# Output weights of the second MLP kept as even columns, then odd ones, with their block sums in freed weight slots on GpSimd's DMA queue

## The chip, the cores and the metric

One Trainium2 chip, one of its cores. The metric is the device time of one execution in microseconds (us); less is better. Engines: PE multiplies matrices (PEld is its weight load, which runs beside the multiplication), DVE, ACT and POOL (GpSimd) compute elementwise, SP only starts transfers. ACT and POOL can start transfers too, each in a queue of its own. Every engine runs its instructions in the order in which they are written.

## The reference, cut to what matters

```python
x = attention(q, k, v, mem_k, mem_v)          # 3072 tokens x 512
x = (sigmoid(x @ w_gate) * (x @ w_val)) @ w_out   # first MLP, 512 -> 1536 -> 512
h = x @ w_in                                  # second MLP, 512 -> 2048
g = h * sigmoid(1.702 * h)
out = g @ w2_out                              # 2048 -> 512, float32
```

All is float32. The kernel multiplies in a shorter format: each operand is cut into a high part (a rounded copy) and a low part (what the copy lost), and a product is three matmuls, high by high, high by low, low by high.

## The kernel before, in words

The tokens are six blocks of 512. Attention and the first MLP fill the first 600 us or so; the second MLP then goes over three pairs of blocks (`sb` 0, 1, 2). Its hidden layer is made for a pair at a time by a seven-product scheme (Strassen's kind): `part_product` (L1366) multiplies weight combinations from a ring (`sb_r`, fetched from `wc_dram` by SP, L1274) with token combinations `sb_x`; ACT copies a bank away (`snap`, L1378, into `sb_s`), DVE adds another bank to the copy (`plus`, L1382), and ACT applies the gate (L1825).

The output product differs by pair:

- For `sb` 0 it is plain. `gemm4` (L790) multiplies with the 16 row blocks f of `w2_out`, once for the first 512 tokens and once for the next, the gated values cut into `gh`, `gl` (`halves`, L1393 on ACT, L1397 on DVE; two buffers of each). Each block lies in a slot of two halves, high and low. The slots of f = 3 to 10 are the two tiles `wq0`, `wq1`, four slots each. A block of the result is copied from its bank into one of two buffers `f2` (L1116, L1118) and stored by SP.
- For `sb` 1 and 2 it is the seven-product scheme again (`b_phase`, from four block pairs j at a time): `b_product` (L1712) takes as its stationary operand 128 of 256 columns of a weight combination. Half s_ = 0 takes the even columns, s_ = 1 the odd ones, so that a later transpose can write the result rows whole:

```python
lhs = w[:, wl * H2 : (wl + 1) * H2].rearrange("p (c z) -> p c z", z=2)[:, :, s_]
```

The weight combinations come from DRAM (`wo_dram`, L1668). `out2` prepares them while the hidden layer of `sb` 0 runs: it converts row block f from float64 (`convert`), keeps the float32 values in `wp_dram` (L1563), and stores three of the seven combinations, which are plain quarters. The other four (m3, m5, m6, m7) are made by `sums2(j)` for the block pairs j = 0 to 7, from the second plain pass on: two loads from `wp_dram` (L1585) into buffers of gated values that are already used up, four sums on DVE (L1594) in the one buffer `sb_t`, two cuts into high (ACT, L1608) and low (DVE, L1611), each of two combinations, and four stores (L1618). All loads and stores are on SP's queue. The first cut's buffer is the half `xl1_g[2:4]`, the second's is `f2`, for every j.

The order on each engine is set by a planner (`Schedule.run`): each step has a cost, keys it reads and writes, and a due time that follows from the products behind it; the planner plays the steps through and writes them down in the order in which it would start them. A waiting step holds everything behind it on its engine.

Of the kernel before, what the change touches and what calls it, by code (L numbers as in the profile page):

```python
# [8 lines left out]
F32 = mybir.dt.float32  # L9
# [6 lines left out]
ALU = mybir.AluOpType  # L16
# [128 lines left out]
def kernel(  # L145
# [112 lines left out]

    sraw = []

    def convert(slot, src, gate=None, put=None, only=None):
# [48 lines left out]

        def join():
            nc.vector.scalar_tensor_tensor(
                out=fi, in0=fi, scalar=3, in1=words()[:, :, 0], op0=ALU.logical_shift_left, op1=ALU.bitwise_or
            )

        def high():
            nc.scalar.activation(slots[slot][:, 0, :], ft, AF.Copy)  # L317

        def low():
            w = slots[slot]  # L320
            eng = nc.vector if low_dve else nc.gpsimd
            eng.tensor_tensor(out=w[:, 1, :], in0=ft, in1=w[:, 0, :].bitcast(F32), op=ALU.subtract)  # L322
# [766 lines left out]
    def gemm4(f, i, banks, row, end=False, tts=range(TT)):  # L1089
# [18 lines left out]
        for tt in tts:  # L1108
# [3 lines left out]
            for c in range(0, 512, h):  # L1112

                def ev(on_dve, c=slice(c, c + h), st=st, bk=bk):
                    if on_dve:
                        nc.vector.tensor_copy(st[:, c], bank[bk][:, c])  # L1116
                    else:
                        nc.scalar.activation(st[:, c], bank[bk][:, c], AF.Copy)  # L1118

                own = c > 0  # L1120

# [434 lines left out]
    def out2(a, b):  # L1556
        for f in range(a, b):
            g = nconv[0] % NF
            sl = slot_out2[f]
            convert(sl, rows(w2_out, f))  # L1560

            def park2(f=f, g=g):
                nc.sync.dma_start(out=wp_dram[f], in_=fts[g])  # L1563
# [12 lines left out]
                add("sp", 0.45, put_, r=r, w=[("wod", unit(j, m), j % 2)], nbytes=P * 512 * 4)  # L1576

    def sums2(j):
        q = 2 if j % 2 == 0 else 6
        wa, wb = (lambda: gbs[q]), (lambda: gbs[q + 1])  # L1580
        ka, kb = ("gB", q), ("gB", q + 1)
        for x in range(2):

            def load(x=x):
                nc.sync.dma_start(out=gbs[q + x], in_=wp_dram[2 * j + x])  # L1585

            add("sp", 0.45, load, r=[("wp", 2 * j + x)], w=[("gB", q + x)], nbytes=P * 512 * 4)
        lo_, hi_ = slice(0, H2), slice(H2, 2 * H2)
        t = lambda: work["t"]
        k0, k1 = ("t", 0), ("t", 1)  # L1590

        def sub(o, x, y, r, op=ALU.subtract):
            def fn():
# [4 lines left out]
        def cut(ms, b_):
            keys = [("gB", 10), ("gB", 11)] if b_ else [("f", NF), ("f", NF + 1)]
            buf = (lambda: twin["l1"][:, 2:4]) if b_ else (lambda: twin["f"])  # L1600

            def part(i, dtype):
                return buf().bitcast(dtype)[:, :, i * H2 : (i + 1) * H2]

            src = lambda: t().rearrange("p (m c) -> p m c", c=H2)
# [24 lines left out]
    GT = ("h0", "l0", "l1", "g3")  # L1630
# [273 lines left out]
```

## Time and profile before

| | us |
|---|---|
| median of three runs | 1159.66 (1158.67 to 1160.36) |
| the profiled execution | 1161.62 |
| its span, first to last instruction | 1159.8 |
| PE busy in the span | 1135.8 |
| DVE, ACT, POOL busy | 811.0, 563.7, 138.8 |

The profile times one execution. What lies outside the span is start and end of the program. Busy time is summed over instructions that overlap only in part, so a busy PE can still be a slow one; the granted clock in a stretch says at which of its two levels (1.2 and 2.4 GHz) it ran there.

### The profile page before, as it was taken

To read this page: it belongs to the slowest core of one execution; us is meant where nothing else is said; L and a number is where in the kernel's file an instruction comes from. 1 tells how busy PE (TensorE), PEld (TensorE's weight loads), DVE (VectorE), ACT (ScalarE), POOL (GpSimd) and SP (SyncE) were. 2 spreads that over 40 slices of the span, in tenths; PEclk is the share of its full clock that TensorE was granted. 3 is DMA by queue.
4 is the path that set the end of the run, shared out by engine and by line. 5 is a ranking of instruction groups with operands and counts; after the bars stand their busy time and mean duration, and the time that the engine had idled before them with its cause. 6 is when DMAs were issued, how large, how long until landed. Compare 5 with 4: busy or idle time off the path is not lost.

```text
span 1159.8 us, 19578 instructions
## 1 busy us (share of the span) xinstructions
PE 1135.8 (98%) x7230; PEld 948.5 (82%) x7230; DVE 811.0 (70%) x1405; ACT 563.7 (49%) x954; POOL 138.8 (12%) x174
## 2 busy tenths in 40 slices
PE   8999999999999999999999999999988999999997
PEld 7888899987888888888888888888866888888886
DVE  7998757776776777878866857648575469675375
ACT  6887622222222323665546677755454365354442
POOL 5322343123233111000000100000000000000000
PEclk9999999999999999999999999999998999999999
DMA  9666344335434424353337777684895576866526
GB/s 207 223 204 191 76 128 94 53 70 126 106 81 84 110 54 124 109 162 120 119 111 248 265 269 259 230 296 146 297 346 199 186 219 205 253 199 192 172 76 179
DMA packets 247791, 196.84 MB, mean 170 GB/s; under 512 B 165136, under 2 KB 191760, under 8 KB 247696
## 3 DMA queue, kind: packets, MB, share of 16 engines
q1 hardware_dynamic: 207624, 173.83, 50.2%
q10 hardware_dynamic: 38152, 15.47, 4.9%
q0 software_dynamic: 1920, 6.29, 1.4%
q8 instruction: 57, 0.93, 0.3%
q14 instruction: 38, 0.31, 0.1%
HBM read 141.00 MB, written 54.53 MB: 169 GB/s over the span
## 4 chain that ended last, share of the span: by engine, by line
PE 90%; DMA 3%; SPq 3%; DVE 1%; ACT 1%; issue 1%; ACTq 0%; DVEq 0%
PE bank L1366 29%; PE bank L1015 15%; PE bank L816 14%; PE bank L1712 14%; PE bank L790 8%; PE bank L823 7%; SPq L345 3%; PE both L699 2%; PE both L550 1%; DMA raw<-in_k_dram 1%; DMA raw<-in_moe_w_in_dram 1%; DMA raw<-in_moe_w_out_dram 0%; PE bank L699 0%; PE bank L880 0%; DMA wo_dram<-xl_g 0%
## 5 line engine op out<-in xcount | busy, mean ns | idle before, releaser
L1366 PE MATMUL bank<-sb_x,sb_r 128*128 128x512 f32 x1512 | 354.6, 393 | 10.8 <-ACT sb_s L1378 10.8
L1366 PEld LDWEIGHTS bank<-sb_x,sb_r 128*128 128x128 f32 x1512 | 286.6, 190 | 72.2 <-ACT sb_s L1378 12.3
L816 PE MATMUL bank<-xh,w 128*128 128x512 f32 (+1 forms) x464 | 159.5, 355 | 0.0
L816 PE MATMUL bank<-xl,w 128*128 128x512 f32 (+1 forms) x464 | 158.6, 353 | 0.1
L1382 DVE TENSOR_TENSOR sb_s<-bank,sb_s 128x512 f32<-128x512 f32 x108 | 74.2, 689 | 74.4 <-PE bank L1366 59.2
L1712 PE MATMUL bank<-wq,w 128*128 128x512 f32 x504 | 123.3, 394 | 0.0
L1712 PEld LDWEIGHTS bank<-wq,w 128*128 128x128 f32 x504 | 97.4, 193 | 20.3 <-ACT wq L1680 0.3
L823 PE MATMUL bank<-xh,w 128*128 128x512 f32 (+1 forms) x464 | 108.8, 356 | 0.0
L1015 PE MATMUL bank<-gh,wq 128*128 128x512 f32 (+1 forms) x448 | 98.8, 361 | 0.0
L816 PEld LDWEIGHTS bank<-xh,w 128*128 128x128 f32 x464 | 87.8, 189 | 12.7
L816 PEld LDWEIGHTS bank<-xl,w 128*128 128x128 f32 x464 | 87.8, 189 | 12.3 <-DVE xl L756 0.5
L1378 ACT ACTIVATE sb_s<-bank 128x512 f32<-128x512 f32 x108 | 64.8, 601 | 52.7 <-PE bank L1366 52.1
L823 PEld LDWEIGHTS bank<-xh,w 128*128 128x128 f32 x464 | 78.2, 189 | 12.3
L1015 PEld LDWEIGHTS bank<-gh,wq 128*128 128x128 f32 x448 | 76.4, 189 | 13.0
L665 DVE STREAM_TRANSPOSE pt<-raw 32x256 f32<-32x256 f32 x184 | 79.6, 432 | 3.7 <-POOL raw L618 1.1
L848 ACT ACTIVATE gh<-sig 128x512 fp32r<-128x512 f32 (+1 forms) x58 | 32.3, 557 | 70.1 <-DVE sig L843 61.6
L618 POOL TENSOR_TENSOR raw<-e,sm 96x448 f32<-96x448 f32 (+2 forms) x69 | 37.9, 560 | 199.3 <-DVE sm L610 163.3
L840 ACT ACTIVATE sig<-bank 128x512 f32<-128x512 f32 (+1 forms) x58 | 30.4, 524 | 61.8 <-PE bank L823 56.5
L322 POOL TENSOR_TENSOR w<-f,w 128x512 fp32r<-128x512 f32 x14 | 20.3, 1452 | 278.3 <-ACT w L317 278.1
L1015 PE MATMUL bank<-gl,wq 128*128 128x512 f32 (+1 forms) x224 | 53.4, 360 | 0.0
L843 DVE SCALAR_TENSOR_TENSOR sig<-sig,bank 128x512 f32<-128x512 f32 (+1 forms) x58 | 34.0, 587 | 26.4 <-PE bank L823 25.1
L567 DVE TENSOR_REDUCE mx<-both 96x8 f32<-96x512 f32 x32 | 21.9, 685 | 40.5 <-ACT xh L753 27.6
(221 smaller groups left out, 1817.4 us busy)
## 6 DMA issues: line engine op xcount, KB each, us to landing
sb_r<-wc_dram SPq DMA_DIRECT2D x133, 256.0 KB
w<-wo_dram SPq DMA_DIRECT2D x42, 512.0 KB
raw<-in_moe_w_out_dram SPq DMA_DIRECT2D x24, 512.0 KB
raw<-in_moe_w_in_dram SPq DMA_DIRECT2D x16, 512.0 KB
wc_dram<-sb_r SPq DMA_DIRECT2D x15, 512.0 KB
w_e<-wo_dram SPq DMA_DIRECT2D x14, 512.0 KB
wf_dram<-f POOLq DMA_DIRECT2D x24, 256.0 KB, 3.2
y_dram<-f ACTq DMA_DIRECT2D x24, 256.0 KB
```

What stands on the lines that cost most here:

```text
L345: add("pool" if pool else "act" if act else "sp", dur, lambda: q_.dma_start(out=dst(), in_=src), r=list(r), w=[key], nbytes=n)
L618: eng.tensor_tensor(out=dst, in0=e3()[r, :, c], in1=T["sm"][r].to_broadcast([n, H, keys[1] - keys[0]]), op=ALU.mult)
L665: nc.vector.transpose(T["pt"][r * CH : (r + 1) * CH, :, c * CH : (c + 1) * CH], T["pn"][c * CH : (c + 1) * CH, :, kb * CH : (kb + 1) * CH],)
L790: nc.tensor.matmul(ps_out, a, c, start=(first and i == 0 and j == 0), stop=(last and i == n - 1 and j == 2),)
L816: nc.tensor.matmul(bank[bk][:, :n], w[:, 0, ts[t]], x[xb][:, t, c0 : c0 + n], start=t == 0 and x is xhs, stop=False)
L823: nc.tensor.matmul(bank[bk][:, :n], w[:, 1, ts[t]], xhs[xb][:, t, c0 : c0 + n], start=False, stop=t == NK - 1)
L843: nc.vector.scalar_tensor_tensor(out=sig[:, :n], in0=sig[:, :n], scalar=1.0, in1=bank[src_val][:, :n], op0=ALU.add, op1=ALU.mult)
L1015: nc.tensor.matmul(bank[into[m]][:, c0 : c0 + n], w[:, wi, m * P : (m + 1) * P], g[:, :n], start=f == 0 and j == 0 and c0 == 0, stop=f == ...
L1366: nc.tensor.matmul(bank[bk], w[:, o : o + P], xt[x, k][:, xl, :], start=first and k == 0 and wl == 0 and xl == 0, stop=k == 1 and wl == 1, ...
L1378: add("act", c_act(BLK), lambda: nc.scalar.activation(work[n], bank[bk], AF.Copy), r=[("bank", bk)], w=[n])
L1382: nc.vector.tensor_tensor(out=work[n], in0=bank[bk], in1=work[n], op=ALU.add)
L1712: nc.tensor.matmul(bank[bk], lhs, quad[b_][:, x, gl_, :], start=begin, stop=last and x == js[-1] and wl == 1, skip_group_check=not first,)
```

## The change: what it does

Four edits, in one diff.

1. `convert(..., split=True)` for the blocks of `w2_out`: the high and low parts are written with the even columns of each 256 first, then the odd ones. The source is read with a step of two elements. The stationary operand of L1712 is then 128 neighbouring columns.
2. `gemm4` of `sb` 0 now yields its columns in that order, so its copies out of the banks write with a step of two elements (`apart(st)`).
3. `sums2` works in weight slots that the second plain pass has used up: j even takes the slots of f = 3 (loaded pair), 4 and 5 (cuts) with `sb_t`; j odd those of f = 6, 7 and 8 with the first gate buffer `sig` in place of `sb_t`. So there are two sets of buffers in place of one. The cuts regroup the columns, reading with a step of two.
4. The pair's two loads become one transfer of 512 KB and each cut's two stores become one of 512 KB, all on POOL's queue, with 4 us of slack in the planner's due times. That is 24 transfers for 48.

```diff
+    def apart(x):
+        return x.rearrange("p (h c s) -> p h s c", s=2, c=P)
...
         def high():
-            nc.scalar.activation(slots[slot][:, 0, :], ft, AF.Copy)
+            w, x = slots[slot][:, 0, :], ft
+            if split:
+                w, x = w.rearrange("p (h s c) -> p h s c", s=2, c=P), apart(ft)
+            nc.scalar.activation(w, x, AF.Copy)
...
+                    x = bank[bk].rearrange("p (h s c) -> p h s c", s=2, c=P)
                     if on_dve:
-                        nc.vector.tensor_copy(st[:, c], bank[bk][:, c])
+                        nc.vector.tensor_copy(apart(st), x)
...
     def sums2(j):
-        q = 2 if j % 2 == 0 else 6
-        wa, wb = (lambda: gbs[q]), (lambda: gbs[q + 1])
-        for x in range(2):
-            def load(x=x):
-                nc.sync.dma_start(out=gbs[q + x], in_=wp_dram[2 * j + x])
+        s_in, *s_out = [sl for g4 in quads4 for sl in g4][3 * (j % 2) : 3 * (j % 2) + 3]
+        def load():
+            nc.gpsimd.dma_start(out=slots[s_in].bitcast(F32), in_=wp_dram[2 * j : 2 * j + 2].rearrange("x p c -> p x c"))
+        add("pool", 1.0, load, r=[("wp", 2 * j), ("wp", 2 * j + 1)], w=wkeys(s_in), nbytes=2 * P * 512 * 4, slack=4.0)
...
-        t = lambda: work["t"]
+        t = (lambda: sigs[0]) if j % 2 else (lambda: work["t"])
...
-                def store(i=i, m=m):
-                    nc.sync.dma_start(out=wo_dram[unit(j, m)][:, j % 2, :], in_=buf()[:, i])
+            def store():
+                dst = wo_dram[u : u + d + 1 : d, :, j % 2, :].rearrange("m p c -> p m c")
+                nc.gpsimd.dma_start(out=dst, in_=slots[sl].bitcast(F32))
...
-        cut(("m5", "m6"), 1)
+        cut(("m6", "m5"), s_out[0])
...
-        cut(("m3", "m7"), 0)
+        cut(("m7", "m3"), s_out[1])
...
-                    lhs = w[:, wl * H2 : (wl + 1) * H2].rearrange("p (c z) -> p c z", z=2)[:, :, s_]
+                    lhs = w[:, wl * H2 : (wl + 1) * H2][:, s_ * P : (s_ + 1) * P]
```

Lines below L240 move down by three to eleven: L1378 becomes L1388, L1397 L1407, L1594 L1604, L1608 L1617, L1611 L1620, L1680 L1691, L1712 L1723, L1825 L1836; the loads of `sums2` are L1595 and its stores L1627. On SP, DVE and ACT nothing is in another order before the second plain pass. Three places change in what the engines wait for.

ACT, before, in the last products of `sb` 1 that come ahead of the first `b_phase` (j = 2 and 3 of the hidden layer; `sb_s` is a bank's copy, `xl_g<-sb_t` and `f<-sb_t` are cuts of `sums2`):

```order
L1825 ACTIVATE xh_g<-bank_5268 128x512
L1680 ACTIVATE wq_746<-xh_g 128x512
L1608 ACTIVATE f_83<-sb_t 128x2x256
L1608 ACTIVATE xl_g<-sb_t 128x2x256
L1825 ACTIVATE xh_g<-sb_s_5303 128x512
L1378 ACTIVATE sb_s_5303<-bank_69 128x512
L1680 ACTIVATE wq_745<-xh_g 128x512
L1825 ACTIVATE xh_g<-sb_s_5303 128x512
L1608 ACTIVATE f_83<-sb_t 128x2x256
L1680 ACTIVATE wq_745<-xh_g 128x512
L1378 ACTIVATE sb_s_5303<-bank_5268 128x512
L1608 ACTIVATE xl_g<-sb_t 128x2x256
```

ACT, in the change, around the last two cuts of `sums2` (the rows `wq_746<-sig`; `L1388` is a bank's copy, `L1836` the gate):

```order
L1388 ACTIVATE sb_s_5303<-bank_5268 128x512
L1617 ACTIVATE wq_746<-sig 128x2x256
L1836 ACTIVATE xh_g<-bank_69 128x512
L1388 ACTIVATE sb_s_5305<-bank_5269 128x512
L1617 ACTIVATE wq_746<-sig 128x2x256
L1128 ACTIVATE f_83<-bank_70 128x2x2x128
L1388 ACTIVATE sb_s_5304<-bank_5268 128x512
L1836 ACTIVATE xh_g<-sb_s_5303 128x512
L1836 ACTIVATE xl_g<-sb_s_5304 128x512
L1836 ACTIVATE xl_g<-sb_s_5305 128x512
L1388 ACTIVATE sb_s_5303<-bank_69 128x512
L1836 ACTIVATE xh_g<-bank_5268 128x512
```

Before, eight of the sixteen cuts stand behind the first `L1680` row, the cuts of the output phase; in the change all sixteen stand ahead of every `L1691` row, the last one in j = 2's products.

DVE, before, in the second plain pass, from the low part of f = 8 to that of f = 12 (`gl` is a low part; `sb_t` a sum of `sums2`):

```order
L1397 TENSOR_TENSOR gl_88<-xl_g,gh_86 128x512
L1249 TENSOR_TENSOR f_81<-sb_y_7584 128x512
L1249 TENSOR_TENSOR sb_y_7584<-sb_y_7585,sb_y_7584 128x512
L1397 TENSOR_TENSOR gl_89<-xl_g,gh_87 128x512
L1397 TENSOR_TENSOR gl_88<-xl_g,gh_86 128x512
L1397 TENSOR_TENSOR gl_89<-xl_g,gh_87 128x512
L1611 TENSOR_TENSOR xl_g<-sb_t,xl_g 128x2x256
L1594 TENSOR_TENSOR sb_t<-xh_g,sb_t 128x256
L1397 TENSOR_TENSOR gl_88<-sb_h_5436,gh_86 128x512
```

DVE, in the change, from the low part of f = 9 to that of f = 11:

```order
L1407 TENSOR_TENSOR gl_89<-xl_g,gh_87 128x512
L1259 TENSOR_TENSOR sb_y_7584<-sb_y_7585,sb_y_7584 128x512
L1604 TENSOR_TENSOR sig<-wq_745 128x256
L1407 TENSOR_TENSOR gl_88<-xl_g,gh_86 128x512
L1604 TENSOR_TENSOR sig<-sig,wq_745 128x256
L1604 TENSOR_TENSOR sb_t<-wq_745 128x256
L1604 TENSOR_TENSOR sb_t<-sb_t,wq_745 128x256
L1620 TENSOR_TENSOR wq_746<-sig,wq_746 128x2x256
L1604 TENSOR_TENSOR sig<-wq_745,sig 128x256
L1620 TENSOR_TENSOR wq_745<-sb_t,wq_745 128x2x256
L1604 TENSOR_TENSOR sig<-wq_745 128x256
L1407 TENSOR_TENSOR gl_89<-xl_g,gh_87 128x512
```

Sums of j = 1 and j = 2 now stand between the low parts that the plain pass needs, so a pair that is not loaded yet holds those up. On PE one product of `sb` 1 (`sb_x00` by `sb_r0`) moves to between f = 8 and f = 9 of the plain pass.

SP, before, near the end of the products (the fetches of `sb_r` wait for free places in the ring; stores of `sums2` between them):

```order
L1618 DMA wo_dram<-xl_g 128x512 x2
L1274 DMA sb_r_4713<-wc_dram 128x512
L1274 DMA sb_r_4464<-wc_dram 128x512
L1618 DMA wo_dram<-f_83 128x512 x2
L1274 DMA sb_r_4523<-wc_dram 128x512
L1274 DMA sb_r_4691<-wc_dram 128x512
L1618 DMA wo_dram<-xl_g 128x512 x2
```

POOL, in the change, its last rows (before, POOL ends with conversions and starts no transfer after the first MLP):

```order
L1627 DMA wo_dram<-wq_746 128x2x512
L1595 DMA wq_745<-wp_dram 128x2x512
L1627 DMA wo_dram<-wq_745 128x2x512
L1627 DMA wo_dram<-wq_746 128x2x512
L1595 DMA wq_745<-wp_dram 128x2x512
L1627 DMA wo_dram<-wq_746 128x2x512
L1627 DMA wo_dram<-wq_745 128x2x512 x2
L1627 DMA wo_dram<-wq_746 128x2x512 x2
```

The stores no longer stand behind ring fetches.

## Rows read from the trace of the kernel before

**Rows 1.** The page's head and its first part: busy us, share, instructions.
```profile
span 1159.8 us, 19578 instructions
PE 1135.8 (98%) x7230; PEld 948.5 (82%) x7230; DVE 811.0 (70%) x1405; ACT 563.7 (49%) x954; POOL 138.8 (12%) x174
```

**Rows 2.** Windows: busy us by engine, granted clock, DMA share, GB/s.
```profile
800.00:820.00 20.00, 20.00 (x90) 16.54 (x90) 12.37 (x21) 7.31 (x12) 0.00 (x0) 1.00 0.43 144
...
840.00:860.00 20.00, 20.00 (x90) 16.58 (x89) 16.07 (x24) 9.95 (x16) 0.00 (x0) 1.00 1.01 357
860.00:880.00 20.00, 9.87 (x35) 7.33 (x33) 9.86 (x18) 8.02 (x15) 0.00 (x0) 0.80 0.77 267
880.00:900.00 20.00, 19.58 (x74) 16.00 (x75) 12.67 (x14) 11.02 (x17) 0.00 (x0) 0.86 0.61 199
```

**Rows 3.** Timeline of PE: start, length, what, count, idle before and releaser.
```profile
836.30 26.00 PE L1366 MATMUL bank<-sb_x,sb_r 128*128 128x512 f32 x114
...
867.91 7.56 PE L1366 MATMUL bank<-sb_x,sb_r 128*128 128x512 f32 x24 [5.61 <-ACT sb_s L1378]
880.42 6.72 PE L1366 MATMUL bank<-sb_x,sb_r 128*128 128x512 f32 x18 [4.95 <-ACT sb_s L1378]
886.98 1.56 PE L1712 MATMUL bank<-wq,w 128*128 128x512 f32 x6
```

**Rows 4.** The chain that ended last, in order of time: start, length, what.
```profile
859.11 5.09 DMA wo_dram<-xl_g
...
873.62 4.87 DMA wo_dram<-f
```

**Rows 5.** Timeline of DVE and SP's queue, 870 to 876 us.
```profile
870.02 0.69 DVE L1611 TENSOR_TENSOR f<-sb_t,f 128x512 fp32r<-128x512 f32 x1 [0.84 <-ACT f L1608]
...
870.87 2.22 SPq L1274 DMA_DIRECT2D sb_r<-wc_dram  x2
...
873.19 0.86 SPq L1618 DMA_DIRECT2D wo_dram<-f  x2
```

**Rows 6.** Timeline of PEld in full stretches of each product.
```profile
904.92 6.96 PEld L1712 LDWEIGHTS bank<-wq,w 128*128 128x128 f32 x30
...
999.18 35.33 PEld L1366 LDWEIGHTS bank<-sb_x,sb_r 128*128 128x128 f32 x156
```

**Rows 7.** Weight loads by line and shape: count, busy us, mean ns.
```profile
L1366 PEld LDWEIGHTS bank<-sb_x,sb_r 128*128 128x128 f32 x1512 | 286.6, 190 | 72.2 <-ACT sb_s L1378 12.3
L1712 PEld LDWEIGHTS bank<-wq,w 128*128 128x128 f32 x504 | 97.4, 193 | 20.3 <-ACT wq L1680 0.3
...
L1712 PEld LDWEIGHTS bank<-wq,w_e 128*128 128x128 f32 x168 | 32.5, 193 | 6.7
```

**Rows 8.** POOL's transfers of L345: issue ns min/median/max, us to landing.
```profile
L345 POOL DMA_DIRECT2D wf_dram<-f x24: 557/580/710, 144.7 to 366.9; - x24
...
DMA to landing us min/median/max: 2.3/3.2/4.5
```

**Rows 9.** POOL's whole queue on the page: packets and MB.
```profile
q0 software_dynamic: 1920, 6.29, 1.4%
```

**Rows 10.** Single lines, ns min/median/max: step-two reading, dense reading.
```profile
L293 ACT ACTIVATE f<-raw x56: 638/668/734, 28.0 to 758.9; 128x512 f32<-128x512 f32 x56
...
L317 ACT ACTIVATE w<-f x33: 613/633/725, 35.0 to 753.6; 128x512 fp32r<-128x512 f32 x33
...
L312 DVE SCALAR_TENSOR_TENSOR f<-f,raw x56: 674/692/1447, 33.3 to 759.6; 128x512 int32<-128x512 int32 x56
...
L322 DVE TENSOR_TENSOR w<-f,w x19: 672/685/1790, 35.6 to 754.3; 128x512 fp32r<-128x512 f32 x19
```

**Rows 11.** Timeline of the plain pass, 811 to 816 us.
```profile
811.83 0.62 PE L790 MATMUL bank<-wq,gh 128*128 128x512 f32 x2
...
812.46 0.69 DVE L1397 TENSOR_TENSOR gl<-xl_g,gh 128x512 fp32r<-128x512 f32 x1 [2.03 <-ACT gh L1393]
...
814.54 0.62 PE L790 MATMUL bank<-xh_w,gh 128*128 128x512 f32 x2
...
814.58 0.43 DVE L1594 TENSOR_TENSOR sb_t<-xh_g,sb_t 128x256 f32<-128x256 f32 x1
```

More of the change, by code (lines that the diff above doesn't have):

```diff
@@ L259, with convert @@
     sraw = []
-    def convert(slot, src, gate=None, put=None, only=None):
+    def convert(slot, src, gate=None, put=None, only=None, split=False):
         u = nconv[0]
@@ L321, in low @@
             eng = nc.vector if low_dve else nc.gpsimd
-            eng.tensor_tensor(out=w[:, 1, :], in0=ft, in1=w[:, 0, :].bitcast(F32), op=ALU.subtract)
+            x, h = ft, [w[:, i, :] for i in range(2)]
+            if split:
+                x, h = apart(ft), [i.rearrange("p (h s c) -> p h s c", s=2, c=P) for i in h]
+            eng.tensor_tensor(out=h[1], in0=x, in1=h[0].bitcast(F32), op=ALU.subtract)
         gate = [gate] if gate else []
@@ L1114, in ev @@
                 def ev(on_dve, c=slice(c, c + h), st=st, bk=bk):
+                    x = bank[bk].rearrange("p (h s c) -> p h s c", s=2, c=P)
                     if on_dve:
-                        nc.vector.tensor_copy(st[:, c], bank[bk][:, c])
+                        nc.vector.tensor_copy(apart(st), x)
                     else:
-                        nc.scalar.activation(st[:, c], bank[bk][:, c], AF.Copy)
+                        nc.scalar.activation(apart(st), x, AF.Copy)
                 own = c > 0
@@ L1559, in out2 @@
             sl = slot_out2[f]
-            convert(sl, rows(w2_out, f))
+            convert(sl, rows(w2_out, f), split=True)
             def park2(f=f, g=g):
@@ L1578, in sums2 @@
     def sums2(j):
-        q = 2 if j % 2 == 0 else 6
-        wa, wb = (lambda: gbs[q]), (lambda: gbs[q + 1])
-        ka, kb = ("gB", q), ("gB", q + 1)
-        for x in range(2):
-            def load(x=x):
-                nc.sync.dma_start(out=gbs[q + x], in_=wp_dram[2 * j + x])
-            add("sp", 0.45, load, r=[("wp", 2 * j + x)], w=[("gB", q + x)], nbytes=P * 512 * 4)
+        s_in, *s_out = [sl for g4 in quads4 for sl in g4][3 * (j % 2) : 3 * (j % 2) + 3]
+        wkeys = lambda sl: [("w", sl, 0), ("w", sl, 1)]
+        wa, wb = (lambda: slots[s_in].bitcast(F32)[:, 0]), (lambda: slots[s_in].bitcast(F32)[:, 1])
+        ka = kb = ("w", s_in, 0)
+        def load():
+            nc.gpsimd.dma_start(out=slots[s_in].bitcast(F32), in_=wp_dram[2 * j : 2 * j + 2].rearrange("x p c -> p x c"))
+        add("pool", 1.0, load, r=[("wp", 2 * j), ("wp", 2 * j + 1)], w=wkeys(s_in), nbytes=2 * P * 512 * 4, slack=4.0)
         lo_, hi_ = slice(0, H2), slice(H2, 2 * H2)
-        t = lambda: work["t"]
-        k0, k1 = ("t", 0), ("t", 1)
+        t = (lambda: sigs[0]) if j % 2 else (lambda: work["t"])
+        k0, k1 = [("sig" if j % 2 else "t", h) for h in range(2)]
         def sub(o, x, y, r, op=ALU.subtract):
@@ L1596, in sub, with cut, part @@
             add("dve", c_dve(H2), fn, r=r, w=[k1 if o.start else k0])
[L1598 to L1605, printed above, removed]
+        def cut(ms, sl):
+            keys = wkeys(sl)
+            def part(i):
+                return slots[sl][:, :, i * H2 : (i + 1) * H2].rearrange("p m (s c) -> p m s c", s=2)
+            src = lambda: t().rearrange("p (m c s) -> p m s c", s=2, c=P)
@@ L1607, in hi @@
             def hi():
-                nc.scalar.activation(part(0, F32R), src(), AF.Copy)
+                nc.scalar.activation(part(0), src(), AF.Copy)
             def lo():
-                nc.vector.tensor_tensor(out=part(1, F32R), in0=src(), in1=part(0, F32), op=ALU.subtract)
+                nc.vector.tensor_tensor(out=part(1), in0=src(), in1=part(0).bitcast(F32), op=ALU.subtract)
+            u = unit(j, ms[0])
+            d = unit(j, ms[1]) - u
+            def store():
+                dst = wo_dram[u : u + d + 1 : d, :, j % 2, :].rearrange("m p c -> p m c")
+                nc.gpsimd.dma_start(out=dst, in_=slots[sl].bitcast(F32))
@@ L1613, in cut @@
             add("act", c_act(512), hi, r=[k0, k1], w=keys)
             add("dve", c_dve(512), lo, r=[k0, k1], w=keys)
-            for i, m in enumerate(ms):
-                def store(i=i, m=m):
-                    nc.sync.dma_start(out=wo_dram[unit(j, m)][:, j % 2, :], in_=buf()[:, i])
-                add("sp", 0.45, store, r=keys, w=[("wod", unit(j, m), j % 2)], nbytes=P * 512 * 4)
-        sub(lo_, lambda: wa()[:, hi_], lambda: wb()[:, hi_], [ka, kb], ALU.add)
-        sub(hi_, lambda: t()[:, lo_], lambda: wa()[:, lo_], [k0, ka])
@@ L1624, in sums2 @@
-        cut(("m5", "m6"), 1)
-        sub(lo_, lambda: wb()[:, lo_], lambda: t()[:, hi_], [k1, kb])
-        sub(hi_, lambda: wa()[:, lo_], lambda: wa()[:, hi_], [ka])
-        cut(("m3", "m7"), 0)
+            add("pool", 1.0, store, r=keys, w=[("wod", unit(j, m), j % 2) for m in ms], nbytes=2 * P * 512 * 4, slack=4.0)
+        sub(hi_, lambda: wa()[:, hi_], lambda: wb()[:, hi_], [ka], ALU.add)
+        sub(lo_, lambda: t()[:, hi_], lambda: wa()[:, lo_], [k1, ka])
+        cut(("m6", "m5"), s_out[0])
@@ L1629 @@
+        sub(hi_, lambda: wb()[:, lo_], lambda: t()[:, lo_], [k0, ka])
+        sub(lo_, lambda: wa()[:, lo_], lambda: wa()[:, hi_], [ka])
+        cut(("m7", "m3"), s_out[1])
     tmps, acc, wos = {}, {}, {}
```

## The prediction

> **What bounds the kernel now.** I read the page's first part, then windows of 20 us, then the timelines of the window that stood out. PE is busy 1135.8 of 1159.8 us [rows 1], so only two things can shorten the run by much: idle or slow time of PE, and fewer or shorter matmuls. From 620 us to the end one stretch alone has idle or slow PE: busy 9.87 of 20 us with the granted clock at 0.80, then 19.58 at 0.86 [rows 2]. The timeline of PE shows it whole: `L1366` starts at 836.30, PE waits 5.61 us, runs 24 matmuls in 7.56 us, waits 4.95 us, runs 18 in 6.72 us, and the output product starts at 886.98; both waits end with ACT's copy of a bank, `L1378` [rows 3]. A full stretch of this product has 156 weight loads in 35.33 us [rows 6], (35.33 - 0.19) / 155 = 0.2267 us each. The stretch holds 114 + 24 + 18 = 156 matmuls, 35.4 us of work, and took 886.98 - 836.30 = 50.7 us. It loses **15.3 us**: 10.6 us of waits and 4.7 us in which the two pieces after them ran at the lower of the two clock levels (0.315 and 0.373 us a matmul).
>
> Why the copies were late is in the chain: two waits of 5.09 and 4.87 us for a store of `sums2` to land [rows 4]. ACT stood before a cut whose buffer was not yet stored, and the bank copies stood behind it. The stores were late for two reasons. SP's queue: the low part was done at 870.02 + 0.69 = 870.7, but its store began at 873.19, behind two ring fetches [rows 5]. And the DMA engines were full (share 1.01 from 840 to 860, against 0.43 from 800 to 820 [rows 2]). With one buffer for each cut, every pair j pays that landing twice over.
>
> **The change part by part.** Lines are those of the kernel before.
>
> *Weight columns.* A full stretch of `L1712` has 30 loads in 6.96 us, (6.96 - 0.19) / 29 = 0.2334 us each, against 0.2267 [rows 6]. The weight load itself means 193 ns in both groups of `L1712`, and 190 in `L1366`, which includes its slow pieces [rows 7]. Tiles, shapes and clock are the same; the step of two is the only difference that I see. There are 504 + 168 = 672 such matmuls [rows 7], 672 x 0.0067 = **4.5 us**, all in a gapless part of PE. Bounds: 0, if something else than the step makes the difference, and 4.5.
>
> The Trainium skill (SBUF — State Buffer, Door 1: The DMA port swizzle) states that accesses which stay in one 16-byte line keep full bandwidth, so that float32 may be strided up to 4 for free. By it this edit would give nothing. The trace does not agree as far as it goes: 6.7 ns a matmul between the steps of one and two.
>
> *The stall.* The change takes away both reasons: stores leave SP's queue, and two sets of buffers double the time from a store to the next cut into the same slot. Moreover the order has all sixteen cuts ahead of the output phase's own cuts, while eight stood behind them. Worth 15.3 us if no bank copy waits again.
>
> *Step-two passes.* ACT reading with a step of two takes 668 ns where dense reading takes 633, DVE 692 against 685 [rows 10]. 16 high parts, 16 cuts and 4 copies on ACT are 36 x 0.035 = 1.3 us, and less on DVE (16 x 0.007 in the cuts). Both are far from full in these stretches (7.31 and 12.37 of 20 us [rows 2]), and nothing there ends late for PE: cost 0, or 1.3 us without that cover. The trace shows no step-two writing of float32 out of a bank and no step-two reading on POOL; from below I take 0, from above twice a pass (0.7 us for 8 copies on two engines, 1.3 us for 5 conversions on a POOL that is idle there). Nobody waits for them closely, so 0.
>
> *POOL's transfers.* Issuing 256 KB took 0.58 us on POOL and landing 2.3 to 4.5 us [rows 8], with 1920 / 24 = 80 packets each [rows 9]. The new ones are 512 KB in 256 runs of 2 KB. Issue: from 0.58 us (no dependence on size) to 0.58 x 256 / 80 = 1.9 us (by packets); I take 1.2. Landing: 256 KB more at the 357 GB/s of the full engines [rows 2] are 0.7 us, so 3.0 to 5.2 us, and up to the 5 us that stores took in full engines plus that, 6. POOL's 24 issues are 14 to 45 us of an engine that otherwise has nothing to do after its last conversion.
>
> *The new waits in the plain pass.* Sums now stand on DVE between low parts that `L790` needs, so a late load holds up `gl`, and with it PE. I follow the tightest place. PE begins f = 11 at 814.54 [rows 11]; the product moved ahead of f = 9 adds 6 x 0.2267 = 1.4, so 815.9. Each f is 12 matmuls, 2.72 us, so f = 6 ends at 803.7. The load for j = 1 needs f = 6's slot and stands behind the first store, whose low part DVE has done at about 803.0 (it stands right after `gl` of f = 7, which needs `gh` and PE's f = 5). So it is issued at about 804.2 and landed at 807.2 to 809.4. The load for j = 2 waits for the last sum of j = 0, about 805.8, and is landed at 808.8 to 811.0 (812 with slow issues). From there on DVE: two sums (0.43 each [rows 11]), a low part (0.69 [rows 10]), a sum, a low part, a sum, `gl` of f = 11: 4 x 0.45 + 3 x 0.65 = 3.8 us, so 814.8 with landing at 811.0, and 815.8 at the late end. PE needs `gl` with its third matmul, at 815.9 + 0.45 = 816.3. It holds by 1.5 us, by 0.5 at the late end. Before, that `gl` was done at 813.15 for 814.54, a margin of 1.4 [rows 11], so this is not thinner; but now it hangs on a landing. The later pairs have 2 us or more by the same steps, and the last pair's stores are landed near 858, ahead of the output phase's cuts into those slots at about 865. I take **0.5 us** of new waits, bounds 0 and 6.
>
> *Sum*, on the profiled execution: 1161.62 - 15.3 - 4.5 + 0.5 = 1142.3. It lies 1.96 us over the median of the runs shown; on the median, 1159.66 - 19.3 = 1140.4, and I forecast **1140.5 us**.
>
> **The rivals.**
>
> *A new wait in the plain pass* (chance 0.15). Landings of 7 us or more, or an issue near 2 us, use up the 1.5 us; each later pair then starts late too, and ACT and DVE hold PE for 3 to 12 us, with some of the clock lost as before (4.7 us went with 10.6). For it: after 822 four fetches of 512 KB join, and stores in full engines took 5 us [rows 4]. Against it: the engines are 0.43 full there [rows 2]. Time: 1144 to 1154.
>
> *The step of two is not the cause of 6.7 ns* (0.08). Then only the stall goes: 1159.66 - 15.3 + 0.5 = 1144.9. For it: the operand of `L1712` comes from other tiles as well. Against it: every load of neighbouring columns, from whatever tile, is at the other rate. The page's rule named above would give this time.
>
> *Part of the old stall stays* (0.06). The DMA engines carry the same bytes; if their share near 1.0 and not SP's order made the landings late, ACT waits again from 836 on, with two sets of buffers for about half as long: 1159.66 - 7.5 - 4.5 = 1147.7.
>
> *Slower: POOL cannot keep up* (0.04). All 24 transfers are issued in order between 795 and 865, 2.9 us for each. Beyond that the last stores are late for the slots of `wq0` and `wq1`, and the output phase waits; the gains of 19.8 us are gone when issues cost (70 + 19.8) / 24 = 3.7 us each. Against it stands 0.58 us [rows 8]; at 4.5 us each it would be 1159.66 - 19.8 + 24 x 4.5 - 70 = 1178.
>
> The Trainium skill (DMA: Bandwidth & Descriptors, SWDGE vs HWDGE vs iDMA) tells of a way to it: POOL writes its descriptors into memory that DVE can lock it out of in some modes. The 24 issues of the trace, with 557 to 710 ns, show no such hold.
>
> *The time stays where it was* (0.02): both terms are lost to new waits.
>
> **How the numbers follow.** The forecast's own case has 0.65: 1139.0 (no new wait, 0.7 for the spread of the runs) to 1143.5 (3 us of waits). Adding the case without the step's gain, and new waits up to 8 us, about half of that rival, gives 0.65 + 0.08 + 0.08 = 0.81: **1139 to 1148 us**. The runs shown spread 0.15%, so 0.2% (2.3 us) is about what can be told from no change. Faster by more than that: 0.65 + 0.15 + 0.08 + 0.06 = 0.94; within it 0.02; slower 0.04.
>
> **What the profile after would show.** Right: PE without an idle time over 1 us between 780 and the last product, granted clock 1.00 in every window there, `L1712`'s successor at 0.2267 us a load, and no wait of ACT for `wo_dram` in the chain. Wrong: waits of PE for `gh` or `gl` (`L790`) or of DVE for `wq<-wp_dram` in the plain pass; POOL's issues well over 1.9 us; weight loads still at 193 ns; or idle PE ahead of the first output product, released by a cut into `wq`.

## The result, and the profile after

The change takes **1145.05 us** (median of 4, 1144.06 to 1145.76) against 1159.86 in the same series: a ratio of 0.9873, 95% interval 0.9856 to 0.989. Its profiled execution took 1145.76 us. The page's head, first part and POOL's queue, for [rows 1, 9]:

```profile
span 1143.7 us, 19549 instructions
PE 1127.6 (99%) x7230; PEld 941.6 (82%) x7230; DVE 809.3 (71%) x1405; ACT 564.6 (49%) x954; POOL 157.1 (14%) x198
...
q0 software_dynamic: 5376, 18.88, 4.5%
```

The span is 16.1 us shorter. The windows that answer to [rows 2] (PE, PEld, DVE, ACT, POOL busy, granted clock, DMA share, GB/s):

```profile
800.00:820.00 20.00, 20.00 (x88) 16.27 (x88) 16.34 (x33) 9.33 (x15) 5.84 (x8) 1.00 0.76 248
820.00:840.00 20.00, 17.89 (x79) 14.52 (x78) 11.82 (x24) 7.17 (x13) 5.83 (x8) 1.00 0.99 353
840.00:860.00 20.00, 20.00 (x90) 16.54 (x89) 11.91 (x21) 12.38 (x22) 5.10 (x7) 1.00 1.03 387
860.00:880.00 20.00, 20.00 (x90) 16.53 (x89) 13.07 (x15) 11.60 (x19) 0.00 (x0) 1.00 0.72 241
880.00:900.00 20.00, 20.00 (x90) 16.57 (x89) 14.42 (x14) 10.85 (x14) 0.00 (x0) 1.00 0.63 198
```

The old stall is gone: 860 to 900 is full at clock 1.00. A new gap of 2.1 us stands just before 840. The timelines of POOL, DVE, ACT and PE around it:

```profile
827.41 0.73 POOL L1595 DMA_DIRECT2D wq<-wp_dram  x1 [1.35 <-DVE sb_t L1604]
...
836.03 0.42 DVE L1604 TENSOR_TENSOR sig<-wq 128x256 f32<-128x256 f32 x1 [3.80 <-DMA wq<-wp_dram]
...
836.83 0.68 DVE L1392 TENSOR_TENSOR sb_s<-bank,sb_s 128x512 f32<-128x512 f32 x1
...
837.00 0.67 ACT L1617 ACTIVATE wq<-sig 128x512 fp32r<-128x512 f32 x1 [4.10 <-DVE sig L1604]
...
838.31 0.68 DVE L1392 TENSOR_TENSOR sb_s<-bank,sb_s 128x512 f32<-128x512 f32 x1
...
839.05 32.95 PE L1376 MATMUL bank<-sb_x,sb_r 128*128 128x512 f32 x144 [2.11 <-DVE sb_s L1392]
```

Read it upwards: PE waits for a bank that DVE adds to `sb_s`; that addition stands behind the sums of pair j = 5; these wait for a load that POOL issued at 827.41 (0.4 us after the sums of j = 3 had left its slot) and that landed 8.6 us later, at 836.03. The landings are in the answers for the lines of load and store (issue in ns min/median/max; us to landing, loads first, then stores):

```profile
L1595 POOL DMA_DIRECT2D wq<-wp_dram x8: 727/728/760, 796.4 to 842.7; - x8
...
DMA to landing us min/median/max: 4.0/6.3/8.6
...
DMA to landing us min/median/max: 3.1/6.6/8.9
```

The weight loads, for [rows 6, 7], take 188 ns instead of 193, and (6.76 - 0.19) / 29 = 0.2266 us each in a full stretch.

```profile
L1723 PEld LDWEIGHTS bank<-wq,w 128*128 128x128 f32 x504 | 94.4, 188 | 20.7 <-ACT wq L1691 0.6 <-issue 0.5
...
L1723 PEld LDWEIGHTS bank<-wq,w_e 128*128 128x128 f32 x168 | 31.5, 188 | 6.5
...
889.29 6.76 PEld L1723 LDWEIGHTS bank<-wq,w 128*128 128x128 f32 x30
```

One more wait is longer than before, 1.21 us at 669, where the kernel before has 0.22. In twelve further profiles it lies between 0 and 0.9 us, in kernels with and without the new sums: it is the execution's, not the change's.

### The profile page after: what moved, and what is told of

The parts are those of the page before. It is cut to its first block, busy times and chain, and to the rows that moved or that the text cites. A ratio compares the mean times of both kernels' runs of the same rounds, so it can differ in the third digit from the quotient of the medians.

```text
span 1143.7 us, 19549 instructions
## 1 busy us (share of the span) xinstructions
PE 1127.6 (99%) x7230; PEld 941.6 (82%) x7230; DVE 809.3 (71%) x1405; ACT 564.6 (49%) x954; POOL 157.1 (14%) x198
## 4 chain that ended last, share of the span: by engine, by line
PE 91%; DMA 3%; DVE 2%; SPq 1%; issue 1%; ACT 1%; POOL 0%; ACTq 0%; DVEq 0%; POOLq 0%
PE bank L1376 29%; PE bank L1024 15%; PE bank L825 15%; PE bank L1723 12%; PE bank L832 8%; PE bank L799 7%; PE both L708 2%; PE both L559 2%; SPq L354 1%; DMA wq<-wp_dram 1%; DMA wp_dram<-f 1%; DMA qn<-in_q_dram 1%; PE bank L708 0%; DMA w<-wo_dram 0%; PE bank L889 0%
## 5 line engine op out<-in xcount | busy, mean ns | idle before, releaser
L1376 PE MATMUL bank<-sb_x,sb_r 128*128 128x512 f32 x1512 | 350.2, 389 | 3.3 <-DVE sb_s L1392 2.1
L1376 PEld LDWEIGHTS bank<-sb_x,sb_r 128*128 128x128 f32 x1512 | 283.5, 188 | 63.3 <-DVE sb_s L1392 2.5
L1723 PE MATMUL bank<-wq,w 128*128 128x512 f32 x504 | 120.5, 389 | 0.3 <-DMA w<-wo_dram 0.2
L1723 PEld LDWEIGHTS bank<-wq,w 128*128 128x128 f32 x504 | 94.4, 188 | 20.7 <-ACT wq L1691 0.6
L825 PEld LDWEIGHTS bank<-xl,w 128*128 128x128 f32 x464 | 87.8, 189 | 11.9
L1388 ACT ACTIVATE sb_s<-bank 128x512 f32<-128x512 f32 x108 | 64.8, 601 | 51.8 <-PE bank L1376 51.2
```

The source lines that it names most:

```text
L825: nc.tensor.matmul(bank[bk][:, :n], w[:, 0, ts[t]], x[xb][:, t, c0 : c0 + n], start=t == 0 and x is xhs, stop=False)
L1376: nc.tensor.matmul(bank[bk], w[:, o : o + P], xt[x, k][:, xl, :], start=first and k == 0 and wl == 0 and xl == 0, stop=k == 1 and wl == 1, ...
L1388: add("act", c_act(BLK), lambda: nc.scalar.activation(work[n], bank[bk], AF.Copy), r=[("bank", bk)], w=[n])
L1723: nc.tensor.matmul(bank[bk], lhs, quad[b_][:, x, gl_, :], start=begin, stop=last and x == js[-1] and wl == 1, skip_group_check=not first,)
```

## The experiments

| kernel | us, median | ratio to before, 95% interval |
|---|---|---|
| column order alone | 1156.35 | 0.9967, 0.9954 to 0.998 |
| sums alone | 1150.18 | 0.9915, 0.9899 to 0.9932 |
| the change again | 1145.72 | 0.9877, 0.9863 to 0.9892 |
| later fetches | 1148.91 | 0.9903, 0.9887 to 0.9918 |
| four load slots | 1145.49 | 0.9868, 0.9853 to 0.9882 |
| loads on SP | 1142.16 | 0.9839, 0.9824 to 0.9854 |
| stores on SP | 1144.51 | 0.9861, 0.9845 to 0.9878 |
| all on SP | 1142.63, again 1142.40 | 0.9843, 0.9829 to 0.9858; 0.9844, 0.9829 to 0.9858 |
| all on SP, four load slots | 1143.05 | 0.985, 0.9835 to 0.9864 |
| one set, on POOL | 1151.09 | 0.9916, 0.9896 to 0.9935 |
| one set, all on SP | 1141.70 | 0.9836, 0.9819 to 0.9852 |

The kernel before took 1160.3 to 1160.7 us in these series.

**The column order alone**: the change with the old `sums2`, whose cuts write the new order.

```diff
-                return buf().bitcast(dtype)[:, :, i * H2 : (i + 1) * H2]
+                return buf().bitcast(dtype)[:, :, i * H2 : (i + 1) * H2].rearrange("p m (s c) -> p m s c", s=2)
...
-            src = lambda: t().rearrange("p (m c) -> p m c", c=H2)
+            src = lambda: t().rearrange("p (m c s) -> p m s c", s=2, c=P)
```

> The column order alone: weights of the second MLP's output are kept as even columns, then odd ones, and the weight loads read them at step one; the block sums keep their old buffers, their order of work and SP's queue, and only their cuts write the new column order. Theory (the weight-load term of the prediction and the stall are two separate things): all weight loads of the output products fall from 193 to 188 ns, the steady pace from 0.2334 to 0.2267 us, 672 of them give 4.5 us, so 1155.2 us, ratio 0.9961; the stall between 836 and 887 us stays as it was (10.6 us of waits and the lower clock level). Rival 1 (the step of two is not what made these loads longer): loads stay at 193 ns, time 1159.9. Rival 2 (the shorter loads only lengthen the stall, since the stored sums come no sooner): 1157 to 1160 with loads at 188 ns.

4.3 us were saved (1160.66 - 1156.35). Its weight loads, and its timelines of SP, ACT and PE:

```profile
L1722 PEld LDWEIGHTS bank<-wq,w 128*128 128x128 f32 x504 | 94.5, 188 | 20.1 <-ACT wq L1690 0.4
```

```profile
814.10 0.80 SPq L1628 DMA_DIRECT2D wo_dram<-xl_g  x2
...
859.75 0.63 ACT L1690 ACTIVATE wq<-xh_g 128x512 fp32r<-128x512 f32 x1
...
863.13 0.66 ACT L1618 ACTIVATE xl_g<-sb_t 128x512 fp32r<-128x512 f32 x1 [2.18 <-DMA wo_dram<-xl_g]
...
866.78 8.29 PE L1376 MATMUL bank<-sb_x,sb_r 128*128 128x512 f32 x24 [4.97 <-ACT sb_s L1388]
...
877.82 0.66 ACT L1618 ACTIVATE f<-sb_t 128x512 fp32r<-128x512 f32 x1 [3.72 <-DMA wo_dram<-f]
...
879.68 5.68 PE L1376 MATMUL bank<-sb_x,sb_r 128*128 128x512 f32 x18 [4.61 <-ACT sb_s L1388]
```

Both rivals fall: the loads are shorter with the step gone, and the stall stays beside them, not longer than before. It is 4.97 + 4.61 of waits and 2.9 + 1.6 of slow matmuls here, 14.0 us against 15.3. Cuts of the output phase (L1690) stand among the sums' cuts (L1618), as in the kernel before.

**The sums alone**: the change with natural columns, read at step two.

```diff
-                    lhs = w[:, wl * H2 : (wl + 1) * H2][:, s_ * P : (s_ + 1) * P]
+                    lhs = w[:, wl * H2 : (wl + 1) * H2].rearrange("p (c z) -> p c z", z=2)[:, :, s_]
```

> The block sums alone: they sit in the weights' slots, two sets by turns, in the new order of the differences and on POOL's queue, while the weights keep their natural columns and are read at step two. Theory: the stall of 836 to 887 us is gone (15.3 us of the profiled time) and the two new waits of the changed kernel (2.1 us near 839 and 1.0 near 669) stand as they do there, weight loads take 193 ns: 1145.05 plus 4.5 = 1149.5 us, ratio 0.991. If the wait near 669 us is a matter of the one execution that was profiled, it is not in this profile. Rival (the column order also shortened the cuts or the evictions that the sums wait for, so that part of the stall's end is its doing): over 1151 us, with waits of PE left between 840 and 890.

1150.18 us, 4.5 more than the change beside it (1145.72), at 193 ns a load. The two parts add up, and the new wait stands here too:

```profile
L1722 PEld LDWEIGHTS bank<-wq,w 128*128 128x128 f32 x504 | 97.2, 193 | 20.9 <-ACT wq L1690 0.7
...
837.45 32.73 PE L1375 MATMUL bank<-sb_x,sb_r 128*128 128x512 f32 x143 [2.88 <-DVE sb_s L1391]
```

**The change again**, unedited.

> The changed kernel once more, for a second profile. If the waits of PE at 839 us (2.1 us, after the 8.6 us landing of the sixth pair's load) and at 669 us (1.2 us, where the kernel before has 0.2) belong to the change, both stand in this profile too, within 0.5 us; if they are chance of one execution, one or both are gone or elsewhere. Time 1145.

The wait at 839 came again, 2.60 us; that at 669 did not. This time the granted clock fell behind it: 130 matmuls took 31.42 us, 1.9 more than at 0.2267.

```profile
838.89 31.42 PE L1376 MATMUL bank<-sb_x,sb_r 128*128 128x512 f32 x130 [2.60 <-DVE sb_s L1392]
```

**Later fetches.** In the change, SP starts three of the first four 512 KB fetches of stored weights from 824.7 on (the fourth left at 811.26), and ring fetches to 834.6, just around that load. The edit holds these fetches back until the seventh pair's first store.

```diff
-                wo_fetch(0)
-                wo_fetch(1)
+                wo_fetch(0, [("wod", unit(6, "m6"), 6 % 2)])
+                wo_fetch(1, [("wod", unit(6, "m6"), 6 % 2)])
```

> The changed kernel, but the first four 512 KB fetches of stored weights (the two prefetched units), which SP issues at 824.7 us just before the load of the sums' sixth pair, wait for the seventh pair's first store. Theory (that load takes 8.6 us instead of 4 to 6 because these fetches, the ring's and the stores fill the DMA engines at a busy share of 0.99): the load lands in about 6 us, the 2.1 us wait of PE at 839 us is gone, time 1145.05 - 2 = 1143, ratio about 0.9855 to the kernel before. Rival 1 (the load is slowed by the sums' own stores and the ring's fetches): no change, 1145, wait still there. Rival 2 (the fetches now come too late for the first output products, or fill the engines under a later pair): the wait moves to after 840 us, 1145 to 1149.

```profile
825.19 0.73 POOL L1595 DMA_DIRECT2D wq<-wp_dram  x1 [0.88 <-DVE sb_t L1604]
...
831.06 0.42 DVE L1604 TENSOR_TENSOR sig<-wq 128x256 f32<-128x256 f32 x1 [1.80 <-DMA wq<-wp_dram]
...
843.66 26.59 PE L1376 MATMUL bank<-sb_x,sb_r 128*128 128x512 f32 x105 [3.78 <-ACT sb_s L1388]
```

The load now lands in 5.9 us, which fits that these fetches were part of its 8.6; but it also left 2.2 us sooner, and the planner put the sums in another order, so that share is not shown. Rival 2 holds: the next pairs pay. PE waits 0.62 us at 835 and 3.78 at 844, the clock is 0.83 in that window, and the kernel is 3 us slower than the change.

**Four load slots**: two further slots for loads, so that these need not wait for the sums of the pair before the last.

```diff
-        s_in, *s_out = [sl for g4 in quads4 for sl in g4][3 * (j % 2) : 3 * (j % 2) + 3]
+        q8 = [sl for g4 in quads4 for sl in g4]
+        s_in, s_out = q8[(0, 3, 6, 7)[j % 4]], q8[3 * (j % 2) + 1 : 3 * (j % 2) + 3]
```

> The changed kernel with four slots instead of two for the sums' loads (the two further ones are slots that stand unused by then); cuts and stores keep their two sets. The load of the sixth pair then need not wait for the differences of the fourth; it is issued some 5 to 9 us sooner, before the four 512 KB fetches at 824.7. Theory (the wait at 839 is that load's landing of 8.6 us): PE's wait of 2.1 to 2.6 us near 839 is gone, 1143, ratio to the kernel before 0.9857. Rival 1 (the same bytes in the same 35 us: with the DMA engines at a busy share of 0.99, something else comes as late): a wait of 1 to 4 us elsewhere between 820 and 860, 1144 to 1149.

My theory fell. The load of j = 5 is early now, and the wait is there all the same, because a cut waits for its slot's store, and stores took up to 11.3 us to land:

```profile
834.38 0.66 ACT L1618 ACTIVATE wq<-sb_t 128x512 fp32r<-128x512 f32 x1 [5.14 <-DMA wo_dram<-wq]
...
838.28 22.08 PE L1376 MATMUL bank<-sb_x,sb_r 128*128 128x512 f32 x89 [2.89 <-DVE sb_s L1392]
```

```profile
DMA to landing us min/median/max: 3.3/6.0/11.3
```

**Which queue.** Loads, stores or both go to SP:

```diff
-            nc.gpsimd.dma_start(out=slots[s_in].bitcast(F32), in_=wp_dram[2 * j : 2 * j + 2].rearrange("x p c -> p x c"))
+            nc.sync.dma_start(out=slots[s_in].bitcast(F32), in_=wp_dram[2 * j : 2 * j + 2].rearrange("x p c -> p x c"))
...
-        add("pool", 1.0, load, r=
+        add("sp", 0.45, load, r=
```

(and the same two lines of `store`). Both on SP:

> The changed kernel with the block sums' 512 KB transfers on SP's queue instead of POOL's; the two sets of slots, the new order of the differences and the column order stay. SP issues in order, and five ring fetches held its sequencer for 8.0 us near 826. Theory (it is mainly the two sets of slots that ended the old stall, the queue only keeps the sums' waits out of SP's way): the old stall's 15 us stay away for the most part, but transfers that wait on the sums now hold the ring's fetches and the outputs' stores behind them, so waits of PE of 2 to 8 us between 820 and 870: 1147 to 1153. Rival 1 (the queue is what ended the stall): 1156 or more, with waits of about 10 us near 860. Rival 2 (the queue is indifferent): 1145.

> The changed kernel with the sums' transfers on SP's queue, once more in five rounds, since it is the fastest so far beside the one with loads alone on SP. Theory (POOL's queue cost the change about 2.5 us): 1142.6, ratio 0.984 to 0.985 to the kernel before, its interval below that of the change (0.9863 to 0.9892). Rival (its median was chance): 1145, ratio 0.987.

Loads alone, then stores alone:

> The changed kernel with only the sums' loads on SP's queue, their stores staying on POOL's. Theory (a load's landing is set by the full DMA engines, not by POOL's queue or its issue of 0.73 us): landing still 5 to 9 us, and the ring's fetches stand behind loads that wait for a slot: 1145 to 1149. Rival (POOL's queue itself makes the landing long): landings of 3 to 4.5 us as SP's 512 KB fetches have when the engines are less full, and 1143.

> The other half of the split: the sums' stores on SP's queue, their loads alone on POOL's, so that no load has a store ahead of it in its queue. Theory A (the wait near 839 came because POOL's queue is in order and a load stood behind stores that waited for their cuts; with everything on SP the load of the sixth pair was issued at 821.0, with everything on POOL at 827.4): loads go out as soon as their slot is free, the sixth by 823, no wait of PE near 839, 1142 to 1143. Theory B (a transfer that POOL issues comes later, 0.73 us of issue and a longer landing): the wait stays, 1145. Rival C (stores that wait for their cuts hold the ring's fetches on SP): a wait of PE on the ring, 1144 to 1150.

I had expected SP to be worse; it is better. All on SP saves another 2.4 to 3.3 us, with no wait of PE from 680 to the output product. Its window around the old wait:

```profile
820.00:840.00 20.00, 20.00 (x90) 16.38 (x89) 13.46 (x27) 9.49 (x16) 0.00 (x0) 1.00 1.04 380
```

With loads alone on SP, every row of DVE, ACT and PE stands in the same order as in the change, so the two differ in transfers alone. In the other edits of slots and queues the planner also put DVE's and ACT's rows into another order. Here the first sums of j = 1, 3 and 5 begin at 809.69, 820.49 and 832.24, in the change at 811.31, 822.62 and 836.03: 1.6, 2.1 and 3.8 us later. The load of j = 5 left SP at 825.25, 2.2 us sooner, and the sums and additions behind it ran in time. The load of j = 6 needed 11.9 us to land even so, and PE did not wait for it:

```profile
825.25 0.56 SPq L1595 DMA_DIRECT2D wq<-wp_dram  x1
...
829.30 0.37 SPq L1595 DMA_DIRECT2D wq<-wp_dram  x1
...
832.24 0.42 DVE L1604 TENSOR_TENSOR sig<-wq 128x256 f32<-128x256 f32 x1
...
836.87 9.46 PE L1376 MATMUL bank<-sb_x,sb_r 128*128 128x512 f32 x41
...
841.17 0.43 DVE L1604 TENSOR_TENSOR sb_t<-wq 128x256 f32<-128x256 f32 x1 [3.06 <-DMA wq<-wp_dram]
```

With stores on SP and loads alone on POOL, the load of j = 5 took 4.4 us, and the wait at 839 is gone, as theory A has it. A's time is not there: 1144.51 against 1142 to 1143, and 2.1 us more than all on SP in the same series. PE waits 0.89 us for a low part that stands behind sums whose load took 6.0 us (815.97 to 821.98), and 1.13 us for a bank copy that stands behind a cut whose slot's store had not landed. Neither wait ends at the ring, as C would have it. Over all eight, the loads alone in POOL's queue land no sooner than with the stores, in 6.2 us for 6.3 (median) and 8.3 for 8.6 (longest):

```profile
825.62 0.72 POOL L1595 DMA_DIRECT2D wq<-wp_dram  x1 [6.33 <-DMA wo_dram<-wq]
...
830.06 0.43 DVE L1604 TENSOR_TENSOR sig<-wq 128x256 f32<-128x256 f32 x1 [1.04 <-DMA wq<-wp_dram]
...
843.53 16.85 PE L1376 MATMUL bank<-sb_x,sb_r 128*128 128x512 f32 x73 [1.13 <-ACT sb_s L1388]
```

```profile
DMA to landing us min/median/max: 4.0/6.2/8.3
```

The four kernels of loads by stores thus part by the loads: 1142.2 to 1142.6 with loads on SP, 1144.5 to 1145.7 with loads on POOL, wherever the stores are.

Four load slots on SP as well (both edits above):

> All of the sums' transfers on SP's queue and four slots for the loads. With SP's queue alone no wait of PE over 0.3 us was left between 680 and 1100. Theory (nothing is left to gain there, since no engine that PE waits for is late): 1142.6, the same as with two load slots within 0.2%. Rival (loads issued earlier push the full DMA engines' other transfers, the cuts wait for the stores of the pair before the last, as they did with four load slots on POOL): 1144 to 1147.

1143.05: nothing more to gain, as the theory had it, with waits of 0.33 and 0.48 us.

**One set** for all pairs instead of two by turns, on POOL and, with the edits above, on SP:

```diff
-        s_in, *s_out = [sl for g4 in quads4 for sl in g4][3 * (j % 2) : 3 * (j % 2) + 3]
+        s_in, *s_out = [sl for g4 in quads4 for sl in g4][0:3]
...
-        t = (lambda: sigs[0]) if j % 2 else (lambda: work["t"])
-        k0, k1 = [("sig" if j % 2 else "t", h) for h in range(2)]
+        t = lambda: work["t"]
+        k0, k1 = ("t", 0), ("t", 1)
```

> The changed kernel with one set of three slots and one buffer of differences for all eight pairs instead of two sets by turns, still on POOL's queue. Each pair then waits for the transfers of the pair ahead: a landing of 6.3 us and some 3.5 us of differences and cuts, about 10 us a pair, 80 us for eight from 796 on, against the 59 us that the changed kernel takes. Theory (the two sets end the old stall): the sums end near 876 and the first output product waits again, 1152 to 1162. Rival (one set on a queue of its own would do): 1145 to 1148.

> The fourth cell of queue by sets: the changed kernel with its sums' transfers on SP's queue and one set of slots and one buffer of differences for all pairs. Two sets gave 1145 on POOL's queue and 1142.5 on SP's, one set on POOL's 1151. Theory (two sets are what keeps a pair's transfers from waiting for the pair ahead; with one set SP's in-order queue also holds ring fetches behind those waits): 1152 to 1160, later than one set on POOL's queue. Rival 1 (SP's queue is the better one whatever the sets): 1147 to 1150. Rival 2 (sets matter only on POOL): 1143.

On POOL the second set is worth 6 us; with one set the last two stores leave at 880.30 and 883.11, ACT waits 3.27 us for a store before its first output cut (885.25), and the first output product waits for that cut. PE also waits 1.37 us for a low part at 814.56, and the granted clock is 0.91 from 880 to 900. On SP the second set is worth nothing (1141.70): rival 2, and my theory was 10 us off. The same load, of j = 1, and what ends each kernel's sums, on POOL:

```profile
805.08 0.74 POOL L1595 DMA_DIRECT2D wq<-wp_dram  x1 [1.14 <-DVE sb_t L1604]
...
813.02 0.42 DVE L1604 TENSOR_TENSOR sb_t<-wq 128x256 f32<-128x256 f32 x1 [4.50 <-DMA wq<-wp_dram]
...
886.35 0.50 PE L1723 MATMUL bank<-wq,w 128*128 128x512 f32 x1 [2.05 <-ACT wq L1691]
```

and on SP:

```profile
802.57 0.37 SPq L1627 DMA_DIRECT2D wo_dram<-wq  x1
...
804.44 0.37 SPq L1595 DMA_DIRECT2D wq<-wp_dram  x1
...
808.98 0.42 DVE L1604 TENSOR_TENSOR sb_t<-wq 128x256 f32<-128x256 f32 x1
...
836.23 43.77 PE L1376 MATMUL bank<-sb_x,sb_r 128*128 128x512 f32 x192
...
875.59 1.06 ACT L1691 ACTIVATE wq<-xh_g 128x1024 fp32r<-128x1024 f32 x1 [2.88 <-DMA wo_dram<-wq]
```

This load took 7.9 us to landing on POOL, at most 4.5 on SP, where DVE did not wait for it. From the load of j = 1 to that of j = 7, a pair took 10.8 us on POOL ((870.15 - 805.08) / 6) and 9.5 on SP ((861.63 - 804.44) / 6). On SP the output cut's wait of 2.88 us is covered: the planner puts the first output product later in a kernel with one set, behind 192 matmuls here (836.23 to 879.84) where the kernel before has 156.

## Why the prediction was right, and where it was not

**Weight columns, 4.5 us: right.** 672 loads at the other rate, all of it won: 4.3 and 4.5 us by the two kernels that do half of the change. The rule that a step of two costs nothing (the Trainium skill, SBUF — State Buffer, Door 1: The DMA port swizzle) did not hold for these weight loads: 193 against 188 ns. In both comparisons (the kernel before with the column order alone, the sums alone with the change) the step moves between the weight loads and the passes that write weights and copy results; nothing else that PE reads differs.

**The stall, 15.3 us: the size is right, but the cures that I named were not needed.** The column order alone keeps a stall of 14.0 us; from it to one set on SP are 14.7 us by the medians. But I gave SP's queue and full DMA engines as the reasons for late stores, held single buffers to make each pair pay for them, and named another queue and two sets as the cure. With SP's queue and a single set the stall stays away, at a DMA share of 0.97 to 0.99 from 820 to 880. So the size came out right beside the reasoning, and in that much it was luck. What that kernel keeps of the new sums is what I had put behind "moreover": its slots are free earlier (first store at 802.57, against 814.10 from the gated values' buffers), and the output phase's cuts need them next, so that all sixteen cuts stand ahead of these (the first L1691 at 875.59, against L1690 at 859.75 between L1618). Besides, it keeps the new order of differences, two transfers joined in one, and the planner's slack of 4 us; and its 192 matmuls ahead of the output product are more cover than the kernel before had. In the two profiles with the stall, before and the column order alone, eight of the sixteen cuts stand behind the first output cut; in all twelve with the new sums none does, and none has the stall's two waits of about 5 us. That speaks for the place and the order of the cuts, but place, order of differences, joined transfers and slack were never parted: which of them is enough stays open.

What I said of the 4.7 us of slow matmuls was too strong: the granted clock was 0.74 on average in the first of the two pieces and 0.62 in the second, so only part of each ran at the lower level.

**Step-two passes: right.** ACT's cut took 0.67 us, and nobody was late by it. ACT's copy out of a bank, for which I had no row, took 622 ns (median) with the columns set apart, against 578 before.

**POOL's transfers and the new waits, 0.5 us: the term that was mis-sized.** The issue took 0.73 us, inside the bounds and near the lower one. The landing, put at 3.0 to 5.2 us and 6 at most, was 4.0 to 8.6 for loads and up to 8.9 for stores. I had set the DMA share of 0.43 against long landings, but that row is of a kernel without these transfers: with them it was 0.76 from 800 to 820, and 0.99 in the 20 us behind. The tight place that I followed just held, as the timelines of DVE and PE of the change show:

```profile
811.31 0.42 DVE L1604 TENSOR_TENSOR sig<-wq 128x256 f32<-128x256 f32 x1 [2.25 <-DMA wq<-wp_dram]
...
815.96 0.69 DVE L1407 TENSOR_TENSOR gl<-xl_g,gh 128x512 fp32r<-128x512 f32 x1
...
816.14 0.61 PE L799 MATMUL bank<-xh_w,gh 128*128 128x512 f32 x2
816.70 0.50 PE L799 MATMUL bank<-xh_w,gl 128*128 128x512 f32 x1
```

The load of j = 1 landed at 811.31 instead of 809.4 at the latest, PE began f = 11 at 816.14 (815.9 forecast), and `gl` was ready at 816.65: the 1.5 us of cover were used up, and PE lost 0.1. (Measured like that cover, to PE's third matmul, the kernel before had 1.8 us there, not 1.4, so the place had become thinner.) DVE's waits for `wq<-wp_dram`, which I had named as a sign of being wrong, were there, without much harm yet. "The later pairs have 2 us or more by the same steps" is the sentence that failed, at j = 5, after j = 1 and j = 3 had been 1.6 and 2.1 us later than with the loads on SP: 2.1 and 2.6 us of wait in two executions of the change, 1.9 more by the clock in one. Against the kernels with SP's queue the whole term is 2.4 to 4 us. So the rival of a new wait came true in part: at 839, just behind the plain pass, at the low end of its 1144 to 1154.

With 3 us for that term and 14 to 15.3 for the stall, the median of 1159.86 gives 1143.1 to 1144.4; the rest to 1145.05 I cannot place.

**The slower rival** was far off: 24 issues of 0.73 us, the last at 855.34.

## What to carry to other kernels

Where a buffer comes free, and what must follow in it, can set the order of the work around it; when a stall ends after an edit that changes place, queue and depth together, undo them one by one before naming the cause. A queue of its own is not faster for being empty: it is in order too, and here loads did better on the busier queue, which issues in half the time (0.37 against 0.73 us). A landing read where the engines are half empty need not be the price where the change itself fills them. Around full DMA engines, moving a transfer out of the way of one load moved the wait to another.

## What had not been expected of the hardware

One 512 KB load, that of j = 1 with one set, took longer from POOL's queue than from SP's with the engines about as full (window 800 to 820: share 0.60 and 0.66): 7.9 us against at most 4.5. The first load of the sums took 4.1 against 3.8 us (first load to first sum that waited for it, one set). The Trainium skill (DMA: Bandwidth & Descriptors, Specifications) gives the first byte as some 0.4 us later on POOL's path than on SP's. That agrees with the first load (0.3) and does not cover the 3.4 us. The stores in the same queue are not shown to be the rest: with them moved to SP this load took 4.7 us on POOL, but the median of the eight stayed (6.2 us). Nor were SP's loads always short: that of j = 6 took 11.9 us with the loads on SP, at a share of 1.01 from 820 to 840. Why the loads cost PE less from SP stays open.

The granted clock did not follow the length of a wait alone: 2.11 and 2.88 us of idle PE (the change, the sums alone) left the window from 840 to 860 at 1.00; 2.60, 2.89 and 3.78 us (the change again, four load slots, later fetches) left it at 0.91, 0.95 and 0.83.
